# A two-branch attention kernel: a quarter of x loaded by a transposing DMA, and the first value projections moved behind the first scores

## The chip, the cores and the metric

The kernel runs on one core of a Trainium2 chip. The core has a matrix engine (TensorE, PE in the profile; its loads of stationary operands are listed apart as PEld), a vector engine (VectorE, DVE), an engine for activation functions (ScalarE, ACT), a general engine (GpSimd, POOL) and an engine that here only issues DMAs (SyncE, SP). Each engine works through its own list of instructions in order, and they wait for one another by semaphores. The metric is the device time of one execution in microseconds; smaller is better.

## What is computed

All of it takes one input `x` of 2048 rows and 512 columns in bf16. Branch A is full softmax attention with 32 heads of 16 columns. Branch B is attention over 8 earlier positions, 2 apart. A gate mixes both row by row.

```python
q, k, v = split(x @ wqkv)                      # 32 heads of 16 columns, A and B with weights of their own
a = softmax(q @ k.T * 16 ** -0.5) @ v @ wo     # branch A: 2048 keys for every query
b = softmax(q . k[pos - 2 * w] * 16 ** -0.5, w = 0..7) @ v[pos - 2 * w] @ wo   # branch B, masked where pos < 2 w
g = sigmoid((x * gate_w).sum(-1))
out = g * a + (1 - g) * b
```

Branch A's scores are 32 x 2048 x 2048 numbers, and each of them needs an exponential.

## The kernel before

**Units, periods and rings.** Scores are made transposed: a unit is one head, 128 keys and 512 queries, that is a tile of 128 x 512 in one PSUM bank. There are 32 heads x 16 key tiles x 4 query chunks = 2048 units. A period is four heads (a head group) and one query chunk, 64 units; there are 32 periods. TensorE writes three units into one ring buffer (`rA`) and two into the other (`rB`), in turns; ScalarE takes the exponential of a whole buffer in one instruction and writes bf16 (`pT`); TensorE multiplies these with the values (`vp_all`) into one accumulator bank (`acc`), which VectorE copies out (`accS`) when a period is over. An instruction of 128x1536 in the profile is an exponential of three units, one of 128x1024 of two.

**Three engines share the exponentials.** A unit can also go to VectorE, which makes the exponential in four passes over integer bits (`dve_unit`: `ta`, `ta`, `ta`, `pd`), or to GpSimd after a copy by VectorE (`pool_unit`: `psc`, `pd`). Such a unit sits in one of two banks called `w`, which the projections use as well.

**The order is made by a planner.** The class `Plan` (lines 52 to 292) is a list scheduler that runs while the program is built. Each job is a generator that asks for an engine, a priority and an assumed duration; the planner starts, at each step, the ready request that can start first, and so writes the order of every engine's list. The hardware then follows these lists and real semaphores. Two constants of it matter here. `limit` (line 185) says until when ScalarE has work, less `refill` (0.4 us); `fits` (line 218) lets a job of lower priority onto TensorE only if it ends within that limit, plus an allowance that grows with the job's waiting time by `RAMP` (0.006 us for each us after `CALM`). Where TensorE would sit idle, `idle_fill` (line 150) puts matmuls with zero weights (fillers: `acc<-ident,z`), which change no result.

**Loading x.** SP issues x in four chunks of 512 rows into `xr` (lines 398 to 407), the last chunk in two halves, with a piece of the query weights between; then the value weights `wv`, the rest of the key and query weights, and the weights of branch B. One piece of the key weights is issued by ScalarE. `x_half` (line 544) then turns half a chunk: eight TensorE transposes of 128 x 128 into a PSUM bank `s`, and one copy into `xT` by VectorE or ScalarE. The table `XDVE` (line 484) says which, and `XARR` (line 485) gives the planner assumed times of arrival. `xT` holds x with its 512 columns on the partitions and feeds every projection.

**The start.** With `xT` of a chunk, `k_job` (line 571) makes the keys of the first head group for that chunk (for the last chunk in two halves); VectorE takes the largest key magnitudes (`kmax_all`), ScalarE writes the keys (`kt_all`). When all five maxima are there, `sel_job` (line 618) makes `selk`, one more TensorE matmul subtracts a bound from the queries (in `q_job`, line 773), and VectorE writes the queries `qt`. Then the first ring can be written. The values of heads 0 to 7 are made by four value jobs (`v_job`, line 741), each of 16 matmuls and one VectorE cast, which `v_group` (line 1632) spawns. On line 1652 they are spawned with no event to wait for, at priority 3. All later value groups wait for the start of a period (`ev_start`).

Of the kernel before, what the change touches and what calls it, by code (L numbers as in the profile page):

```python
# [23 lines left out]
QW = 512  # L24
# [27 lines left out]
class Plan:  # L52
# [13 lines left out]
    held = {"job": 0}  # L66
    streamed = deque()
    cap_job = 2
    refill = 0.4
    patience = 6.0  # L70

    def resource(self, name, n):
# [106 lines left out]

    DEFER = 0.0  # L180
    coming = 0.0
    RAMP = 0.006
    CALM = 4.0

    def limit(self, st):
# [32 lines left out]
    def fits(self, x, st):  # L218
# [3 lines left out]
        give = self.EARLY if st < self.TEARLY else 0.0  # L222
        return st + x[4] - self.limit(st) <= max(give, self.RAMP * (st - x[7] - self.CALM))

# [71 lines left out]
def kernel(  # L296
# [12 lines left out]
    x2d = A_x.flatten_outer_dims()  # L309
    out2d = out.flatten_outer_dims()  # L310
    S, D = x2d.shape
    assert D == 512 and S == 2048
    NT = S // 128
    NC = S // QW
# [41 lines left out]
    SP = Chained(nc.sync, "sp")  # L356
# [16 lines left out]
    xT = const.tile([128, DC, S], BF16, name="xT")  # L373
# [24 lines left out]
    def load_x(t0, n):  # L398
        SP.dma_start(out=xr[t0 // 8][:, t0 // 4 % 2, t0 % 4:t0 % 4 + n],
                     in_=x2d[t0 * 128:(t0 + n) * 128, :].rearrange("(t p) n -> p t n", p=128))  # L400
# [2 lines left out]
    load_x(4, 4)  # L403
    SP.dma_start(out=wqr[:, :, 0:128], in_=a_w3[:, :, 0:128])
    load_x(8, 4)
    load_x(12, 2)
    load_x(14, 2)
    SP.dma_start(out=wv[:], in_=a_w3[:, :, 2 * D:3 * D])
    SP.dma_start(out=wkr[:, :, 128:D], in_=a_w3[:, :, D + 128:2 * D])
    SP.dma_start(out=wqr[:, :, 128:D], in_=a_w3[:, :, 128:D])  # L410
# [70 lines left out]
    THIN = 0.40  # L481
    KRP = 4
    QRP = 3
    XDVE = ((1, 0), (1, 0), (1, 1), (0, 1))
    XARR = ((5.8, 5.8), (7.2, 7.2), (9.3, 9.3), (9.9, 10.6))
    WARR = (4.8, 8.0)
    GP = 4.5
    BB = 3
# [24 lines left out]
    ev_x = [Event() for _ in range(NC)]  # L513
# [7 lines left out]
    ev_start = [Event() for _ in range(NP)]  # L521
# [16 lines left out]

    def x_job(sc):
        left = [2]  # L540
        for hf in range(2):
            yield ("spawn", x_half(sc, hf, left))

    def x_half(sc, hf, left):
        yield ("delay", XARR[sc][hf])
        w = Bank("s")

        def tr(s):
            P.thin = 0.16
            w.open(s, [128, DC, 256], BF16)  # L550
            for tt in range(2):
                for c in range(DC):
                    PE.transpose(out=w.t[:, c, tt * 128:(tt + 1) * 128],
                                 in_=xr[sc // 2][:, sc % 2, 2 * hf + tt, c * 128:(c + 1) * 128], identity=ident[:])
        yield ("pe", 0, 0.45, tr, "s")
        dst = xT[:, :, sc * QW + hf * 256:sc * QW + (hf + 1) * 256]
        if XDVE[sc][hf]:
            yield ("dve", 1, 0.70, lambda: V.tensor_copy(out=dst, in_=w.t[:]))
        else:
            yield ("act", 0, 1.02, lambda: A.copy(out=dst, in_=w.t[:]))  # L560
        yield w.close()
        left[0] -= 1
        if left[0] == 0:
            yield ("set", ev_x[sc])
# [176 lines left out]
    def v_job(h0, h1, tb, TB, rel, prio):  # L741
        n = (h1 - h0) * DH
        if rel is not None:
            yield ("wait", rel)
        for sc in range(tb * 128 // QW, -(-(tb + TB) * 128 // QW)):
            yield ("wait", ev_x[sc])
        w = Bank()

        def pe(t0, t1):
            def f(s=None):  # L750
                if t0 == 0:
                    w.open(s, [128, TB, n])
                for tt in range(t0, t1):
                    for c in range(DC):
                        mm(w.t[:, tt, :], xT[:, c, (tb + tt) * 128:(tb + tt + 1) * 128],
                           wv[:, c, h0 * DH:h1 * DH], c == 0, c == DC - 1)
                P.thin = (t1 - t0) * (one - 4 * n / 2400.0)
            return f
        step = TB if TB < 8 else TB // 2
        one = 4 * max(0.0555, n / 2400.0)  # L760
        for t0 in range(0, TB, step):
            yield ("pe", GO if t0 else prio, one * step + SW, pe(t0, t0 + step)) + (("w",) if t0 == 0 else ())
        yield ("dve", prio, VP, lambda: V.tensor_copy(out=vp_all[:, tb:tb + TB, h0:h1, 0:DH],
                                                      in_=w.t[:].rearrange("p t (h d) -> p t h d", d=DH)))
        yield w.close()
        for t in range(tb, tb + TB):
            for i in range(h0 // 4, h1 // 4):
                yield ("set", ev_v[(i, t)])
                v_left[0] -= 1
# [3 lines left out]
    def q_job(p, rel, prio):  # L773
        c_, i = periods[p]
        if rel is not None:
            yield ("wait", rel)
        yield ("wait", ev_x[c_])
        yield ("wait", ev_wq)
        if p > 0:
            yield ("wait", ev_sel[i])  # L780
        w = Bank()

        def pe(s):
            w.open(s, [128, QW])
            for c in range(DC):
                mm(w.t[:], wqp[:, c, i].rearrange("p j d -> p (j d)"), xT[:, c, c_ * QW:(c_ + 1) * QW],
                   c == 0, c == DC - 1)
        yield ("pe", prio, 4 * MM + SW, pe, "w")
        st = {}

        def absq():
            st["a"] = work.tile([128, QW], BF16, name="absq", tag="absq", bufs=1)
            hi = w.t[:].bitcast(I16).rearrange("p (n two) -> p n two", two=2)[:, :, 1]
            V.tensor_scalar(out=st["a"][:].bitcast(I16), in0=hi, scalar1=0x7FFF, scalar2=None, op0=ALU.bitwise_and)
        if p == 0:
            def absa():
                st["a"] = work.tile([128, QW], BF16, name="absq", tag="absq", bufs=1)
                A.activation(out=st["a"][:], in_=w.t[:], func=ACT.Abs)
            yield ("act", 0.2, 0.69, absa)
        else:  # L800
            yield ("dve", prio, VP, absq)
        yield ("wait", ev_sel[i])
        yield ("pe", GO, MM + SW, lambda: mm(w.t[:], selk_all[:, i, :], st["a"][:], False, True,
                                               skip_group_check=True))

        def evac():
            qt = work.tile([128, QW], BF16, name="qt", tag="qt", bufs=3)
            V.tensor_scalar(out=qt[:], in0=w.t[:], scalar1=QSC, scalar2=qbias[:, 0:1], op0=ALU.mult, op1=ALU.add)
            qt_tiles[p] = qt
        yield ("dve", prio, VP + 0.06, evac)  # L810
        yield w.close()
        yield ("set", ev_q[p])
# [819 lines left out]
    def v_group(h0, h1, rel, prio):  # L1632
        n = (h1 - h0) * DH
        TB = 512 // n
        for tb in range(0, NT, TB):
            P.spawn(v_job(h0, h1, tb, TB, rel, prio + 0.01 * tb))
# [5 lines left out]
    for sc in range(NC):  # L1642
        P.spawn(x_job(sc))
# [5 lines left out]
        P.spawn(k_job(0, NC - 1, None, 1.5, hf))  # L1649
    P.spawn(sel_job(0, 1.5))  # L1650
    P.spawn(q_job(0, None, 1.6))
    v_group(0, 8, None, 3)
    P.spawn(act_stream())
    P.spawn(g_job(GP))
    P.spawn(psc_job(ev_lent), 16.0)
# [79 lines left out]
```

## Time and profile before

Three timed runs took 845.38, 846.5 and 847.3 us, a median of 846.5 us. The profiled execution took 844.47 us, of which 842.7 us are the span of its instructions.

| engine | busy us | share of the span | instructions |
|---|---|---|---|
| PE | 743.3 | 88% | 5798 |
| DVE | 768.6 | 91% | 1333 |
| ACT | 825.7 | 98% | 750 |
| POOL | 731.0 | 87% | 740 |

The first exponential of a ring starts at 17.76 us. The loads of the first 21 us keep the 16 DMA engines busy; after that DMA is busy for a quarter of the time on average. TensorE's granted clock is at full speed in nearly all slices of the page. A busy TensorE is not one at its peak, since its matmuls overlap and since fillers count as busy.

### The profile page before, as it was taken

The numbers are of one execution on the slowest core, as the hardware profiler recorded it, in microseconds if no ns is written. First come the engines' busy times: TensorE is split into PE (matmuls) and PEld (weight loads), VectorE is DVE, ScalarE is ACT, GpSimd is POOL, SyncE is SP. The second block draws the span as 40 slices with busy tenths as digits, with TensorE's granted clock in tenths as the row PEclk, the third lists the DMA queues.
The fourth block names the chain that finished last, engine by engine and source line by source line (L and its number), as shares of the span: only waits on it lengthen the run. The fifth ranks groups of instructions, "written<-read, shape, count | busy, mean of one in ns | idle before, by whom it ended". The sixth has DMA issues, their size and how long they took to land.

```text
span 842.7 us, 15724 instructions
## 1 busy us (share of the span) xinstructions
PE 743.3 (88%) x5798; PEld 266.4 (32%) x5854; DVE 768.6 (91%) x1333; ACT 825.7 (98%) x750; POOL 731.0 (87%) x740
## 2 busy tenths in 40 slices
PE   9999998988898888888899898888898898888897
PEld 5423432333233323332333232332233332232222
DVE  5799999999999999999987999999999989998887
ACT  5999999999999999999999999999999999999996
POOL 2678679998999999999899999999989898978891
PEclk9999999999999999999999999999999999999999
DMA  9003240604243312230233240402212222110000
GB/s 296 7 14 107 89 132 22 208 22 109 92 135 123 98 53 64 75 110 10 70 89 94 64 142 21 131 14 73 84 33 82 69 87 77 26 57 14 8 1 26
DMA packets 72590, 63.85 MB, mean 76 GB/s; under 512 B 20528, under 2 KB 69168, under 8 KB 72512
## 3 DMA queue, kind: packets, MB, share of 16 engines
q1 hardware_dynamic: 71312, 62.57, 24.6%
q8 instruction: 46, 0.75, 0.4%
q10 hardware_dynamic: 1200, 0.26, 0.2%
q14 instruction: 32, 0.26, 0.1%
HBM read 46.14 MB, written 12.62 MB: 70 GB/s over the span
## 4 chain that ended last, share of the span: by engine, by line
ACT 73%; issue 20%; PE 7%; DVE 0%; POOL 0%; ACTq 0%; POOLq 0%
ACT pT L350 71%; PE acc L350 2%; PE ring L350 2%; PE w L350 2%; ACT lg L350 1%; PE s L350 1%; PE e L350 0%; DVE vp_all L350 0%; DVE qt L350 0%; ACT osc L350 0%; POOL ident masks.py:199 0%; ACT e L350 0%; POOL identf masks.py:197 0%; ACTq L350 0%; POOL ident masks.py:197 0%
## 5 line engine op out<-in xcount | busy, mean ns | idle before, releaser
L350 ACT ACTIVATE pT<-ring 128x1536 bf16<-128x1536 f32 x717 | 815.3, 1425 | 2.5 <-PE ring L350 1.8
L350 PE MATMUL ring<-qt,kt_all 32*128 32x512 bf16 x1857 | 286.9, 381 | 87.4 <-ACT pT L350 74.5
L350 DVE SCALAR_TENSOR_TENSOR ta<-ta,w 128x512 f32<-128x512 f32 x476 | 317.2, 681 | 6.1
L350 POOL TENSOR_TENSOR prod<-prod 128x512 f32<-128x512 f32 (+1 forms) x208 | 240.4, 1166 | 5.8
L350 PE MATMUL acc<-pT,vp_all 128*17 128x512 bf16 x1792 | 221.7, 384 | 2.7 <-DVE accS L350 2.4
L350 PEld LDWEIGHTS <-kt_all 32*128 32x128 bf16 x2113 | 114.2, 91 | 337.4 <-issue 325.3
L350 DVE TENSOR_SCALAR ta<-w 128x512 f32<-128x512 uint16 x238 | 162.6, 686 | 37.0 <-PE w L350 34.6
L350 PE MATMUL acc<-ident,z 128*17 128x512 bf16 (+5 forms) x741 | 185.5, 335 | 1.6 <-POOL ident masks.py:199 1.4
L350 DVE SCALAR_TENSOR_TENSOR pd<-ta,w 128x512 uint16<-128x512 f32 x238 | 160.5, 680 | 2.9
L350 POOL TENSOR_TENSOR prod<-ksh,qb 128x512 f32<-128x512 bf16 x128 | 144.8, 1156 | 8.7 <-DMA ksh<-kv_scr 6.4
L350 POOL TENSOR_TENSOR prod<-vsh,lg 128x512 f32<-128x512 bf16 x128 | 136.7, 1098 | 2.4
L350 PE MATMUL w<-qt,kt_all 32*128 32x512 bf16 x256 | 96.4, 383 | 0.1
L350 PE MATMUL acc<-pd,vp_all 128*17 128x512 bf16 x256 | 85.8, 382 | 0.0
L350 PEld LDWEIGHTS <-z 128*17 128x17 bf16 (+1 forms) x749 | 52.5, 91 | 67.8 <-issue 40.6
L350 PEld LDWEIGHTS <-vp_all 128*17 128x17 bf16 x2048 | 40.5, 87 | 93.4 <-issue 93.0
L350 POOL TENSOR_TENSOR psc<-psc 128x512 f32<-128x512 f32 x54 | 64.4, 1193 | 4.2
L350 PE MATMUL w<-bw,xT 128*128 128x512 bf16 x167 | 48.4, 382 | 1.4
L350 POOL TENSOR_SCALAR psc<-psc 128x512 f32<-128x512 uint16 (+1 forms) x36 | 22.2, 618 | 27.8 <-DVE psc L350 24.8
L350 PEld LDWEIGHTS <-xT 128*128 128x128 bf16 x448 | 31.3, 98 | 27.5 <-issue 14.0
L350 POOL TENSOR_TENSOR lg<-lg,mx 128x256 f32<-128x256 f32 x16 | 10.1, 629 | 22.3 <-DVE mx L350 22.3
L350 DVE COPY accS<-acc 128x512 f32<-128x512 f32 (+1 forms) x33 | 22.0, 668 | 1.5 <-PE acc L350 1.4
L350 DVE CAST kvs<-w 128x512 bf16<-128x512 f32 x32 | 21.8, 682 | 1.1 <-PE w L350 1.1
(108 smaller groups left out, 454.3 us busy)
## 6 DMA issues: line engine op xcount, KB each, us to landing
ksh<-kv_scr SPq DMA_DIRECT2D x16, 1024.0 KB
vsh<-kv_scr SPq DMA_DIRECT2D x16, 1024.0 KB
kv_scr<-kvs SPq DMA_DIRECT2D x16, 256.0 KB
kt_all<-k_scr SPq DMA_DIRECT2D x6, 512.0 KB
q_scr<-qpk SPq DMA_DIRECT2D x24, 128.0 KB
qt<-q_scr SPq DMA_DIRECT2D x24, 128.0 KB
out_dram<-osb SPq DMA_DIRECT2D x14, 128.0 KB
xr<-in_A_x_dram SPq DMA_DIRECT2D x3, 512.0 KB
```

Source lines behind the costliest of these rows:

```text
L350: return chain_on(self._key, f(*a, **k))
```

## The change

The last 512 rows of x are no longer loaded into `xr` and turned by TensorE. One transposing DMA, issued by SP in the place of the two half loads, writes them straight into `xT`; for that chunk the planner is told to assume an arrival at 12.6 us. The value jobs of heads 0 to 7 now wait for the event that marks the start of the first period, so they come behind the first scores in the planner's order. Two constants of the planner change: `refill` from 0.4 to 0.52 and `RAMP` from 0.006 to 0.01.

```diff
-    refill = 0.4
+    refill = 0.52
...
-    RAMP = 0.006
+    RAMP = 0.01
...
     load_x(8, 4)
-    load_x(12, 2)
-    load_x(14, 2)
+    SP.dma_start_transpose(out=xT[:, :, 3 * QW:S], in_=x2d[3 * QW:S, :])
     SP.dma_start(out=wv[:], in_=a_w3[:, :, 2 * D:3 * D])
...
-    XDVE = ((1, 0), (1, 0), (1, 1), (0, 1))
-    XARR = ((5.8, 5.8), (7.2, 7.2), (9.3, 9.3), (9.9, 10.6))
+    XDVE = ((1, 0), (1, 0), (1, 1))
+    XARR = ((5.8, 5.8), (7.2, 7.2), (9.3, 9.3), (12.6, 12.6))
...
     def x_job(sc):
         left = [2]
+        if sc == NC - 1:
+            yield ("delay", XARR[sc][0])
+            yield ("set", ev_x[sc])
+            return
         for hf in range(2):
...
-    v_group(0, 8, None, 3)
+    v_group(0, 8, ev_start[0], 3)
```

## The prediction

> **What bounds the kernel now.** I read the page first: busy shares, then the chain that ended last, then the costliest groups. (Columns of a group: its form and count | busy time, mean ns of one | idle before it.)
>
> ```profile
> PE 743.3 (88%) x5798; PEld 266.4 (32%) x5854; DVE 768.6 (91%) x1333; ACT 825.7 (98%) x750; POOL 731.0 (87%) x740
> ACT 73%; issue 20%; PE 7%; DVE 0%; POOL 0%; ACTq 0%; POOLq 0%
> L350 ACT ACTIVATE pT<-ring 128x1536 bf16<-128x1536 f32 x717 | 815.3, 1425 | 2.5 <-PE ring L350 1.8
> ```
>
> ScalarE is 98% busy, 815.3 of its 825.7 us with the 717 exponentials of the score ring, and these wait 2.5 us in all. So the span is three parts: the head up to the first exponential, the exponentials with their gaps, and the tail after the last. Three answers give the parts: ScalarE's timeline, and the exponentials' busy time in chosen stretches (columns: stretch, length, PE busy, ACT busy, clock, DMA share, GB/s).
>
> ```profile
> 17.76 17.32 ACT L350 ACTIVATE pT<-ring 128x1536 bf16<-128x1536 f32 x15 [1.79 <-PE ring L350]
> 836.75 0.37 ACT L350 COPY oT<-e 128x256 bf16<-128x256 bf16 x1 [2.59 <-PE e L350]
> 17.76:34.89 17.13, 3.94 (x35) 17.13 (x15) 1.00 0.23 74
> 747.82:834.16 86.34, 24.14 (x190) 86.13 (x77) 0.98 0.04 12
> ```
>
> Head 17.76 us; exponentials 17.76 to 834.16 = 816.40 us; tail 842.7 - 834.16 = 8.5 us. The pace comes from clean stretches: 38 exponentials (19 pairs of a three-unit and a two-unit one, a unit being 512 columns) between two small ACT operations at 167.24 and 210.11 take 42.87 us, 2.256 us a pair; 15 (8 long, 7 short) take 17.13 us, so a long one costs 17.13 - 7 x 2.256 = 1.34 us and a short one 0.915. The program before has 358 long and 359 short ones: 358 x 1.34 + 359 x 0.915 = 808.2 (a fit of 0.427 a unit plus 0.0615 an instruction gives 808.7). Sixteen `lg` exponentials at 0.31 between neighbours add 5.0, the gate's 0.1. Sum 813.8; the other 2.6 us are small gaps. The largest lies at the last change of accumulator: 76 exponentials from 747.82 should take 37 x 2.256 + 2 x 0.915 = 85.3 and take 86.3, and there TensorE's granted clock falls (clock third from the end):
>
> ```profile
> 811.00:814.00 3.00, 2.28 (x21) 0.65 (x19) 3.00 (x6) 3.00 (x4) 2.75 (x4) 0.84 0.00 0
> 814.00:817.00 3.00, 3.00 (x20) 1.15 (x21) 2.93 (x7) 2.79 (x3) 2.75 (x4) 0.59 0.00 0
> ```
>
> The head's own chain is in TensorE's and VectorE's timelines (start, length, operation, count).
>
> ```profile
> 9.94 2.13 PE L350 MATMUL s<-ident,xr 128*128 128x128 bf16 x32
> 11.90 2.76 PE L350 MATMUL s<-xT,wkp 128*128 128x512 bf16 x16
> 14.81 1.07 PE L350 MATMUL w<-wv,xT 128*128 128x128 bf16 x16
> 17.32 0.39 PE L350 MATMUL ring<-qt,kt_all 32*128 32x512 bf16 x3
> 13.83 1.35 DVE L350 TENSOR_REDUCE kmax_all<-s 128x1 f32<-128x512 f32 x3 [0.17 <-PE s L350]
> 15.41 0.25 DVE L350 TENSOR_SCALAR selk_all<-selq,kmax 128x128 bf16<-128x128 bf16 x1
> 15.91 0.69 DVE L350 CAST vp_all<-w 128x512 bf16<-128x512 f32 x1 [0.25 <-PE w L350]
> 16.52 0.74 DVE L350 TENSOR_SCALAR qt<-w,qbias 128x512 bf16<-128x512 f32 x1
> ```
>
> Transposes of x, keys, maxima, `selk`, then a value group on TensorE and its cast on VectorE ahead of `qt`, then the first ring, whose exponential starts 0.44 later.
>
> **What the skill says.** No x load is transposed by DMA before, but outputs are. The Trainium skill, Advanced Engine Details and Errata, section X-Bar Transpose (TRN2): such DMAs are as fast as regular ones, 350 to 400 GB/s; its page DMA: Bandwidth & Descriptors, section Latency and other measured facts, gives 261 GB/s where the middle dimension isn't contiguous. The trace is lower. A transpose of 128 KB alone on the queues (40 slices of 0.2 us from 128.0):
>
> ```profile
> 128.22 1.20 SPq L350 DMA_TRANSPOSE oT<-otok  x1
> GB/s 0 0 0 0 0 0 0 164 220 210 62 0 0 0 0 0 0 0 0 0 0 0 0 0 0 0 0 0 0 0 0 0 0 0 0 0 0 0 0 0
> ```
>
> It holds SP for 1.20 us, moves nothing for those, then 210 to 220 GB/s. I use 220. That source lies in SBUF, the new one in HBM; 150 and 261 are my bounds. For the clock, the skill's TensorE: Matmul & The Clock Gate (What's actually happening) says that an idle window of about 3.4 us throttles TensorE; the trace agrees so far that the clock fell just where TensorE was 2.28 of 3 us busy.
>
> **Part 1: the transposing load.** It removes two loads, 16 TensorE transposes, one xT copy on ScalarE and one on VectorE. The 32 transposes of 9.94 to 11.90 become 16, so TensorE is 1.0 us ahead. Then I walk on by durations of the rows. Keys of chunk 1: 10.95 to 11.8. Keys of chunk 2 wait for both copies of that chunk, both on VectorE, which in the trace end at 11.9: 12.0 to 12.9. Keys of chunk 3, in two halves of 0.45 (16 matmuls took 2.76, so four 256-wide ones half of 0.87): 12.9 to 13.8, if the transposed data is there. The last maximum ends 0.5 to 0.6 later as before (14.66 to 15.18), at 14.4; `selk` 0.48 after that, as before, at 14.9 against 15.66. Gain so far 0.8.
>
> Is the data there at 12.9? DMA rates in 1 us slices of the first 40 us:
>
> ```profile
> GB/s 0 25 104 325 349 315 91 295 385 361 347 349 327 333 376 400 387 399 368 350 346 99 10 0 0 16 0 0 0 0 0 0 0 0 0 0 0 16 0 0
> ```
>
> To 9.0 us they sum to 1889 KB. Ahead of the transpose stand 131 + 524 + 524 + 131 + 524 = 1834 KB and some 50 KB of instructions, so its turn comes at 9.0; being issued from about 2.9, its 1.2 us of preparation, even four times that (4.8), lie beside those transfers. 524 KB at 220 GB/s are 2.4 us: 11.4. From the last byte to TensorE's first use was 0.5 (second load: 1182 KB at 6.7, use at 7.23) to 1.2 us (first: 4.6, use at 5.80); 0.9 gives 12.3, no wait. At 261 it is 11.9; at 150, 13.4 and 0.5 lost. Queued behind it on SP are `wv`, the other weights and the `zpad` row: `wv` started at 5.54; if SP is held until 10, its 524 KB end by 12.5 at the 340 GB/s of the trace, and it is needed at 16.5. The rest is used tens of microseconds later. Queue delays cost nothing.
>
> **Part 2: values after the first scores.** In the changed program's order the first value group stands behind the first ring. It frees `selk`'s matmul from the group that ended at 15.88, and `qt` from a cast until 16.6. So `selk`'s matmul is at 14.9 to 15.4, `qt` 15.4 to 16.15, ring 16.2, first exponential 16.65: 1.1 before 17.76 in all. Ring, group of 1.0, ring is the pattern that stood at 17.32 to 19.03 and left no gap in 17.13 us; one more such slot is hidden behind the exponentials.
>
> **Part 3: the two planner constants.** `refill` and `RAMP` change no operation's length, but with the new head they reorder every engine's list. Counted there: 359 long and 359 short exponentials, 1795 units against 1792; VectorE has 236 units against 238, GpSimd 17 against 18. That puts 0.427 + 0.915 = 1.34 us onto ScalarE, the bound; VectorE's and GpSimd's relief lies beside it. TensorE has 26 more fillers, put where the plan has it idle: cost nothing. Gaps: 2.6 now. I can bound them only: 0 below (nothing waits), 4.6 above (two more dips like that at 811, of 1.0 each). At the last change of accumulator the new order has ten ring matmuls and five 512-wide fillers where it had six and two, which keeps TensorE busier; I take that dip as mostly gone: 1.9, so -0.7. Tail: behind the last exponential stand 7 matmuls into `acc` for 4, one more wave of 0.21, and two fewer `bwo` ones at the very end: +0.15 (bounds -0.3 and +0.5).
>
> **Sum.** -1.1 + 1.34 - 0.7 + 0.15 = -0.3: span 842.4. The profiled execution took 844.47 device us for its 842.7; the timed ones 845.38 to 847.3, median 846.5, so 3.8 over the span: 846.2.
>
> **Rivals.**
> Faster: the gaps nearly vanish, because the larger `refill` holds back TensorE jobs that end close to the moment ScalarE runs dry. For it: the 26 extra fillers show a slacker TensorE plan. Against: most pieces already run at the floor (67 exponentials from 49.03 in 75.42 us, 33 x 2.256 + 0.915 = 75.36). With 0.6 left: -1.1 + 1.34 - 2.0 + 0.15 = -1.6, and up to 0.4 more if `qt` is sooner: 844.7. The floor with no gap is 16.65 + 808.7 + 1.34 + 5.1 + 8.65 = 840.4, or 844.2.
> Slower: the transpose from HBM lands late. Keys of chunk 3 stand in TensorE's list with everything after them, so each microsecond past 12.9 goes straight to the first exponential. From 14.9 on (105 GB/s) the kernel is over 0.2% slower; at 15.4, which is 16 blocks issued one after another at 0.3 us each only from 9.0 on with 1.6 to the use, it is -0.3 + 2.5 = +2.2: 848.7. For it: nothing here shows an HBM source, and SP is held 1.2 us for a quarter of the bytes. Against: the preparation can lie under the earlier loads.
> Also slower: two more clock dips than now, -1.1 + 1.34 + 2.0 + 0.15 = +2.4: 848.9. That the change does nothing is excluded: 16 transposes are gone and the ring stands first.
>
> **Chances.** Measurement tells this kernel from no change at about 0.2%, 1.7 us. Forecast (within): 0.42. Faster: 0.32. Slower: 0.26, of which late transpose 0.16 and dips 0.10. The forecast's own range is 844.8 to 847.7. The range for 8 in 10 takes in the faster case with 0.4 for scatter, and the slower ones at their named size: 843.8 to 848.9.
>
> **What would show it.** First exponential at 16.65 (right), or above 17.76 with TensorE waiting for the DMA of xT before the chunk 3 keys (wrong). 718 exponentials, sum of their busy time up by 1.3. From the first to the last exponential 817.1 (816.4 + 1.34 - 0.7). No dip of the clock near the end. Wrong if dips appear at other changes of accumulator, or if the sum of gaps leaves 0.6 to 3.5.

## The result, and the profile after

The changed kernel takes 849.57 us (849.07 to 849.78, four runs) against 846.5: a ratio of 1.0036, 95% interval 1.0019 to 1.0054. It is slower, and outside the predicted range of 843.8 to 848.9. The profiled execution spans 848.0 us against 842.7; in the runs of this study the device time is 1.73 to 2.06 us above the span, 1.78 in those four.

First the page of the changed kernel: busy shares, the chain that ended last, and the group of the exponentials (busy time, mean ns | idle before it).

```profile
PE 751.2 (89%) x5813; PEld 267.4 (32%) x5864; DVE 762.1 (90%) x1323; ACT 826.6 (97%) x750; POOL 725.3 (86%) x734
...
ACT 66%; issue 20%; PE 10%; DVE 4%; POOL 0%; ACTq 0%; POOLq 0%
...
L350 ACT ACTIVATE pT<-ring 128x1536 bf16<-128x1536 f32 x718 | 817.2, 1408 | 5.2 <-PE acc L350 2.4
```

There are 718 exponentials, as forecast. They wait 5.2 us where they waited 2.5, the largest part (2.4) for TensorE's `acc`; TensorE's share of the chain rose from 7 to 10%. ScalarE's timeline gives the bounds of the three parts, and one window its busy time in the middle part (columns: stretch, length, PE, PEld, DVE, ACT, POOL busy, clock, DMA share, GB/s).

```profile
17.88 19.53 ACT L350 ACTIVATE pT<-ring 128x1536 bf16<-128x1536 f32 x17 [1.43 <-PE ring L350]
...
818.81 20.45 ACT L350 ACTIVATE pT<-ring 128x1536 bf16<-128x1536 f32 x18 [1.28 <-PE acc L350]
```

```profile
17.88:839.26 821.38, 730.42 (x5683) 257.75 (x5731) 749.59 (x1284) 817.61 (x735) 719.52 (x720) 1.00 0.24 72
```

Head 17.88 (before 17.76), middle 839.26 - 17.88 = 821.38 (816.40), tail 8.74 (8.54). The 5.3 us are in the middle. By the prediction's own measure the work of these exponentials is 813.8 + 1.34 = 815.1, which leaves 6.2 us of gaps against 2.6. (That measure is an estimate, good to about 0.5 us: the prediction's two sums for the exponentials before are 808.2 and 808.7, and its fit as printed gives 809.3. The difference between two kernels hardly depends on it.) ScalarE idles 821.38 - 817.61 = 3.77 us of the middle, against 0.76 before; the rest of the gaps, 2.4 and 1.8 us, is time in which ScalarE is busy, at a pace a little below that of the clean stretch.

The head did shorten, but it started later. TensorE's timeline from the start (start, length, operation, count), of the changed kernel:

```profile
1.44 5.82 PE L350 MATMUL acc<-ident,z 128*32 128x512 bf16 x17 [1.44 <-POOL ident masks.py:199]
7.20 1.07 PE L350 MATMUL s<-ident,xr 128*128 128x128 bf16 x16
...
12.15 2.99 PE L350 MATMUL s<-xT,wkp 128*128 128x512 bf16 x16
...
17.44 0.39 PE L350 MATMUL ring<-qt,kt_all 32*128 32x512 bf16 x3
17.76 1.07 PE L350 MATMUL w<-wv,xT 128*128 128x128 bf16 x16
```

and the same first lines of the kernel before:

```profile
1.44 4.43 PE L350 MATMUL acc<-ident,z 128*32 128x512 bf16 x17 [1.44 <-POOL ident masks.py:199]
5.80 1.07 PE L350 MATMUL s<-ident,xr 128*128 128x128 bf16 x16
```

The 17 fillers ahead of the first transposes took 5.82 us in one execution and 4.43 in the other. A filler of 512 columns took 0.63 us at first and 0.38 later, and the change, TensorE's full clock, came at about 7.0 us here and 4.0 there (the trace's first record of full clock stands at 6.93 and 4.10; ahead of it the clock column reads 1.00 without a record). A second profile of the changed kernel has them done sooner, first transposes at 6.16, first exponential at 16.84. From first transposes to first exponential it is 10.68 us in both, 11.96 and 11.71 in two profiles of before: 1.0 to 1.3 shorter. The keys at 12.15 wait for no DMA. The load can be told apart in the trace by its packets, 2048 of 256 bytes that the kernel before doesn't have: they move from 8.3 to 11.25 us, and the prediction had 9.0 to 11.4. This is SP's queue:

```profile
3.29 6.47 SPq L350 DMA_TRANSPOSE xT<-in_A_x_dram  x1
9.81 0.58 SPq L350 DMA_DIRECT2D wv<-in_A_wqkv_dram  x1
```

Where ScalarE idles in the middle (the bracket is the idle time and its releaser; `818.81` above is the last of them):

```profile
59.16 8.23 ACT L350 ACTIVATE pT<-ring 128x1536 bf16<-128x1536 f32 x7 [0.34 <-PE ring L350]
67.57 7.01 ACT L350 ACTIVATE pT<-ring 128x1024 bf16<-128x1024 f32 x6 [0.18 <-PE ring L350]
75.28 14.58 ACT L350 ACTIVATE pT<-ring 128x1024 bf16<-128x1024 f32 x13 [0.70 <-PE acc L350]
90.39 15.12 ACT L350 ACTIVATE pT<-ring 128x1536 bf16<-128x1536 f32 x13 [0.53 <-PE w L350]
105.73 27.23 ACT L350 ACTIVATE pT<-ring 128x1024 bf16<-128x1024 f32 x24 [0.22 <-PE w L350]
153.76 22.71 ACT L350 ACTIVATE pT<-ring 128x1024 bf16<-128x1024 f32 x20 [0.17 <-PE acc L350]
...
489.00 28.14 ACT L350 ACTIVATE pT<-ring 128x1024 bf16<-128x1024 f32 x25 [0.23 <-PE acc L350]
```

These eight make 3.65 of the 3.77 us. The second profile has all eight at the same distance from its first exponential, and equal within 0.01 us, so they belong to the instruction lists, not to chance. The kernel before has one, 0.32 us, 31 us after its first exponential.

### The profile page after: what moved, and what is told of

Its sections match the earlier page's. It is cut to its first block, busy times and chain, and to the rows that moved or that the text cites. A ratio compares the mean times of both kernels' runs of the same rounds, so it can differ in the third digit from the quotient of the medians.

```text
span 848.0 us, 15723 instructions
## 1 busy us (share of the span) xinstructions
PE 751.2 (89%) x5813; PEld 267.4 (32%) x5864; DVE 762.1 (90%) x1323; ACT 826.6 (97%) x750; POOL 725.3 (86%) x734
## 4 chain that ended last, share of the span: by engine, by line
ACT 66%; issue 20%; PE 10%; DVE 4%; POOL 0%; ACTq 0%; POOLq 0%
ACT pT L350 65%; PE w L350 4%; PE acc L350 3%; PE ring L350 3%; DVE ta L350 2%; ACT lg L350 1%; PE s L350 1%; DVE pd L350 1%; PE e L350 0%; DVE psc L350 0%; DVE xT L350 0%; DVE d L350 0%; DVE kt_all L350 0%; DVE osb L350 0%; DVE omg L350 0%
## 5 line engine op out<-in xcount | busy, mean ns | idle before, releaser
L350 PE MATMUL acc<-ident,z 128*17 128x512 bf16 (+3 forms) x770 | 193.6, 338 | 1.4 <-POOL ident masks.py:199 1.4
L350 PE MATMUL acc<-pd,vp_all 128*17 128x512 bf16 x253 | 82.0, 380 | 0.0
L350 POOL TENSOR_TENSOR psc<-psc 128x512 f32<-128x512 f32 x51 | 60.8, 1193 | 3.9
```

What stands on the lines that cost most here:

```text
L350: return chain_on(self._key, f(*a, **k))
```

## The experiments

Each was compared with the kernel before, in four groups of runs. "Clock" is TensorE's mean granted clock; below, a run "at full clock" is one of at least 0.998. It has to be told apart because two thirds of the runs of before, 24 of 35 in the first group, lie below 0.998 and take 846.8 us, while the other 11 take 845.25 (medians; in the other groups before takes 845.16, 844.92 and 845.26 at full clock, so that 0.3 us between groups mean nothing). All ten timed runs of the changed kernel are at full clock.

| kernel | time us | ratio (95%) | at full clock us (runs) |
|---|---|---|---|
| before, run again | 845.72 | 0.9989 (0.9982, 0.9997) | 844.9 (8) |
| load alone | 845.60 | 0.9993 (0.9980, 1.0005) | 843.9 (4) |
| value wait alone | 850.14 | 1.0044 (1.0029, 1.0059) | 848.8 (1) |
| load and value wait, old constants | 847.84 | 1.0019 (1.0012, 1.0026) | 847.75 (16) |
| the same and RAMP | 847.94 | 1.0018 (1.0010, 1.0026) | 847.9 (15) |
| the same and refill | 848.58 | 1.0024 (1.0017, 1.0031) | 848.6 (13) |
| load and constants, no value wait | 846.78 | 1.0018 (1.0009, 1.0028) | 846.4 (11) |
| the change, again | 849.45 | 1.0034 (1.0021, 1.0047) | 849.45 (6) |
| the change with refill 0.51 | 849.12 | 1.0042 (1.0026, 1.0058) | 848.75 (4) |
| two exchanges in TensorE's list | 849.64 | 1.0038 (1.0023, 1.0053) | 849.6 (5) |
| a wider exchange | 850.10 | 1.0041 (1.0026, 1.0055) | 850.1 (6) |
| load, ten fillers at the start | 844.95 | 0.9974 (0.9964, 0.9984) | 844.0 (4) |
| before, ten fillers at the start | 845.86 | 1.0002 (0.9989, 1.0015) | 844.3 (5) |
| load, ten fillers, values moved by hand | 846.85 | 1.0005 (0.9995, 1.0015) | 845.1 (7) |

And the parts read from each profile: head from the first transposes of x to the first exponential, the middle, its exponentials, the gaps over their work (813.8 for before's 717; 815.1 for 718; 815.6 where a 512-column one makes 719; 816.1 with refill 0.51, where a two-unit one does), ScalarE's idle time in it, and the tail.

| kernel | head | middle | exps | gaps | idle | tail | clock |
|---|---|---|---|---|---|---|---|
| before | 11.96 | 816.40 | 717 | 2.6 | 0.76 | 8.5 | 0.998 |
| before, again | 11.71 | 815.88 | 717 | 2.1 | 0.55 | 8.5 | 1.000 |
| load alone | 11.04 | 818.52 | 717 | 4.7 | 2.66 | 8.5 | 0.994 |
| value wait alone | 11.35 | 822.16 | 719 | 6.5 | 3.89 | 9.0 | 0.992 |
| load and value wait | 10.68 | 819.25 | 719 | 3.6 | 1.33 | 9.0 | 1.000 |
| and RAMP | 10.69 | 819.82 | 719 | 4.2 | 1.79 | 8.9 | 1.000 |
| and refill | 10.84 | 820.21 | 719 | 4.6 | 2.27 | 8.9 | 0.999 |
| load and constants | 11.04 | 818.51 | 719 | 2.9 | 1.13 | 8.6 | 1.000 |
| the change | 10.68 | 821.38 | 718 | 6.2 | 3.77 | 8.7 | 0.999 |
| refill 0.51 | 10.68 | 820.72 | 719 | 4.7 | 2.38 | 9.0 | 0.999 |

### Each part alone

The load alone: the edits of the load, `XDVE`, `XARR` and `x_job`, in the kernel before. Its list differs from before only ahead of the first ring.

> Part 1 of the change alone: the transposing load, the value jobs and both planner constants as before. Its lists differ from those before only ahead of the first ring (16 TensorE transposes and two copies fewer), 717 exponentials as before. Theory A (the planner's new lists cost the time, the load is good): 0.8 to 1.2 us faster than before, the stretch from the first to the last exponential 816 to 817 us. Theory B (the load costs the time, because it holds SP for 6.5 us and leaves holes in the DMA traffic): no gain or slower, the first exponential at 17.9 or later even where TensorE's clock is up early. Theory C (the two profiles differ by when TensorE's clock came up, 4.0 us before and 7.0 after): the first exponential moves by up to 1.4 us from run to run of one kernel, at the same lists.

The value wait alone, in the kernel before:

```diff
-    v_group(0, 8, None, 3)
+    v_group(0, 8, ev_start[0], 3)
```

> Part 2 alone: the value jobs wait for the first period, x is loaded as before, constants as before. The planner writes other lists: 718 exponentials (1795 units), VectorE 235 and GpSimd 17. Theory A: head 0.4 us sooner, 1.3 us more exponential work, and gaps of 2 to 5 us between exponentials: 1 to 4 us slower than before. Theory B: about +0.9 (the 1.3 less 0.4), no more gaps than before.

The changed kernel with the old constants:

```diff
-    refill = 0.52
+    refill = 0.4
-    RAMP = 0.01
+    RAMP = 0.006
```

> Parts 1 and 2 without part 3: the changed kernel with refill 0.4 and RAMP 0.006. Its lists are those of the kernel with part 2 alone but for the head. Theory A: 0.8 to 1.2 us faster than the kernel with part 2 alone, and against the whole change it tells what the constants cost: if they are the cause, 2 us or more faster than the whole change; if the value wait alone throws the lists about, the same as the whole change. Theory B: as slow as the whole change, since the load is in it.

The changed kernel again, unchanged:

> The whole change once more. Theory A: about 3 us slower than before, first to last exponential again 821 us, whatever the head does. Theory C: its first exponential can come at 16.5 to 17.9, depending on when TensorE's clock comes up.

The load did what it was meant to: head 11.04, and at full clock 843.9 us (four runs) against 845.25, 1.35 less; over all runs the gain is within the noise. Of the 2.66 us of idle time in its profile, 2.0 lie where the clock falls. In windows around them (columns as above, clock third from the end) the load alone has

```profile
638.00:641.00 3.00, 2.92 (x16) 0.89 (x16) 1.52 (x5) 2.34 (x3) 2.92 (x3) 0.56 0.22 46
764.00:767.00 3.00, 3.00 (x17) 0.96 (x14) 2.16 (x5) 2.56 (x3) 2.92 (x4) 0.50 0.03 5
767.00:770.00 3.00, 3.00 (x16) 0.51 (x14) 2.38 (x6) 2.07 (x3) 2.40 (x2) 0.50 0.01 3
```

and before, run again, with the same list there:

```profile
638.00:641.00 3.00, 2.86 (x22) 0.98 (x20) 2.51 (x7) 3.00 (x4) 2.84 (x3) 1.00 0.06 12
764.00:767.00 3.00, 2.65 (x25) 1.07 (x20) 2.93 (x6) 3.00 (x4) 2.92 (x4) 1.00 0.01 3
767.00:770.00 3.00, 2.41 (x20) 0.70 (x20) 1.66 (x5) 3.00 (x4) 2.35 (x2) 1.00 0.00 0
```

So the middle of a run at 0.994 may not be set against one at 1.0: that would charge the load with 2.6 us, while its runs at full clock show none. The value wait is the dear part. Added to the load it takes another 0.36 us off the head and puts 3.4 us onto the middle against before run again (819.25 against 815.88): 1.83 of exponential work, because one more long exponential (1.34) and one of 512 columns (0.49 by the prediction's fit) come to ScalarE, and 1.5 of gaps. The tail is 0.5 longer. The value wait alone shows the same list in a run at 0.992: head 11.35, and a middle that the clock has stretched to 822.16. By these profiles it costs 3.5 us in all, by the times at full clock 3.9 (847.75 against 843.9).

### The two constants

Only `refill`, then only `RAMP`, as in the changed kernel, the other one old:

> The changed kernel with RAMP back at 0.006; load, value wait and refill 0.52 stay. Lists: 718 exponentials, 754 fillers, VectorE 235. If refill alone makes the gaps between exponentials (the plan believes TensorE jobs are harmless that are not), first to last exponential is 821 us or more, as with the whole change, against 819.25 with both old constants. If any new list brings gaps of its own by chance, it lies anywhere from 817 to 823 us, at places other than 75, 90 and 818 us.

> The changed kernel with refill back at 0.4; load, value wait and RAMP 0.01 stay. Lists: 718 exponentials, 734 fillers. If RAMP is the cause (it lets TensorE jobs that have waited run past the point where ScalarE runs dry), gaps as with the whole change and 821 us from the first to the last exponential; if refill is, about 819. By chance of the list: anywhere from 817 to 823.

Each on its own costs something, 0.96 and 0.57 us of the middle; by time it is 0.85 and 0.15 at full clock, so `RAMP` alone is hardly told from nothing. Neither reached the 821 us that was set as the sign of a sole cause. `refill` brings, in the place of one of 0.68, the six idle spells of 59 to 154 us, all of them and at the same places; a spell like that of 489 comes with `RAMP`. The largest, 1.28 us at 818.81, is in neither: among these lists it needs both. So the two are no sum of single prices. The constants without the value wait (its line back to `None`) and the changed kernel with `refill` 0.51:

> The changed kernel with its first value group planned as before, ahead of the first scores: the load and the two constants, without the value wait. Its list has 718 exponentials (+1.34 us, as the changed kernel). Theory A (the constants as such reorder TensorE's work so that it comes late for the ring): head about 11.04 us from the first transposes as with the load alone, and from the first to the last exponential at least 820.4, as 819.3 + 1.1 or more; time 848.5 or above. Theory B (each setting gives its own list, good or bad, and only the pairing with the value wait is a bad one): the middle can be anything, 816.5 to 822; a middle below 818.5 and a time below 847 speak for it.

> The changed kernel with refill 0.51 for 0.52: the same parts, another list (719 exponentials, 1797 units against 1795, so 0.9 to 1.8 us more of them). Theory A (refill above 0.5 in general costs gaps): middle 822 to 823.5, as 821.4 with the longer exponentials, gaps about 6. Theory B (what the constant does is a matter of each single list): gaps that differ by 1 us or more from 6.2, either way, and at other places than 57.98 to 152.6 and 818.8.

Without the value wait the same constants leave gaps of 2.9 and three small spells of idle time in the whole middle:

```profile
48.80 75.64 ACT L350 ACTIVATE pT<-ring 128x1024 bf16<-128x1024 f32 x67 [0.32 <-PE acc L350]
...
306.49 27.23 ACT L350 ACTIVATE pT<-ring 128x1024 bf16<-128x1024 f32 x24 [0.32 <-PE acc L350]
486.68 10.06 ACT L350 ACTIVATE pT<-ring 128x1024 bf16<-128x1024 f32 x9 [0.33 <-PE acc L350]
```

Their cost there is the exponential work, +1.83, and 0.8 of gaps. The middle, 818.51, is on the edge that was set for theory B, and the time below its 847: it speaks for B more than for A. With 0.51 the middle, 820.72, is below what A had set. The six early spells stay as they are, within 0.01 us, which B had not expected, while those of 489.00 and 818.81 are gone: B holds for the late part of the list only. A step of 0.01 in a constant moved 1.3 us of idle time and one exponential; at full clock the time fell by 0.7 us only, since the exponentials' work grew by 0.9.

### Is it the order, or TensorE's time?

At 88.92 the changed kernel has a projection of 1.04 us just ahead of a ring, and ScalarE then idles 0.53 until 90.39. That looked like a wrong order. Two kernels put it to the test, with every other instruction of TensorE where it was and the lists of the other engines unchanged.

```diff
+            def go():
                 for c in range(DC):
                     mm(w.t[:], wqr[:, c, 128 * (b + 1):128 * (b + 2)], ...)
+            (put_off if b == 0 and c_ == 0 else now)(go, True)
...
                         qk_mm(ring[:, s_, :], p_, t, j)
+                while late:
+                    late.pop(0)()
```

> The changed kernel with two pairs of neighbours exchanged in TensorE's list by hand, and every other instruction where it was: the third wkr projection (at 73.09 in the changed kernel's profile) and the first wqr projection (at 88.92) each go behind the ring that they stand ahead of. Theory A (the planner put a projection of 1.0 us ahead of a ring that ScalarE needed at once; the order is the cause): the idle 0.53 us at 90.39 is gone, as that exponential waits for nothing but its ring. The idle 0.70 at 75.28 may stay, because the trace names the accumulation at 74.58 as its releaser, and that still stands behind the projection. Middle 820.2 to 820.9 for 821.4. Theory B (TensorE is short of time there, whatever the order): the idle time comes back within the next few exponentials and the middle stays at 821.2 to 821.5.

> As the version before, but the wkr projection goes behind the accumulation that follows the ring too (four matmuls), just ahead of the next ring. Theory A: both the 0.70 and the 0.53 us are gone, middle 820.0 to 820.3, time 1.1 to 1.3 us below the changed kernel, 848.3. Theory B: idle time reappears behind them and the middle stays above 821.

Theory A fell. TensorE with the exchange at that place,

```profile
88.51 0.39 PE L350 MATMUL ring<-qt,kt_all 32*128 32x512 bf16 x3
88.83 1.04 PE L350 MATMUL w<-xT,wqr 128*128 128x512 bf16 x4
89.80 0.39 PE L350 MATMUL w<-qt,kt_all 32*128 32x512 bf16 x1
90.12 0.60 PE L350 MATMUL acc<-pT,vp_all 128*17 128x512 bf16 x5
90.65 0.39 PE L350 MATMUL ring<-qt,kt_all 32*128 32x512 bf16 x2
```

and ScalarE:

```profile
74.79 15.93 ACT L350 ACTIVATE pT<-ring 128x1024 bf16<-128x1024 f32 x14 [0.92 <-PE acc L350]
91.14 1.02 ACT L350 ACTIVATE pT<-ring 128x1024 bf16<-128x1024 f32 x1 [0.42 <-PE ring L350]
92.44 12.86 ACT L350 ACTIVATE pT<-ring 128x1536 bf16<-128x1536 f32 x11 [0.28 <-PE ring L350]
```

The ring is served early, and the next two are late: 0.42 and 0.28 for 0.53, and 0.92 for 0.70. The middle is 821.84, and 822.13 with the wider exchange (0.28 and 0.49 in place of the 0.70), against 821.38; that is above the bounds of B too. At these places a projection that is moved only moves the wait. What else stands there is seen in TensorE's groups from 38 to 76 us after the first exponential (busy us, mean ns | idle before), of before run again:

```profile
L350 PE MATMUL ring<-qt,kt_all 32*128 32x512 bf16 x88 | 13.5, 382 | 2.1 <-ACT pT L350 1.9
...
L350 PE MATMUL w<-bw,xT 128*128 128x512 bf16 x12 | 3.1, 382 | 0.0
L350 PE MATMUL acc<-ident,z 128*17 128x512 bf16 x8 | 3.1, 384 | 0.0
L350 PE MATMUL w<-wv,xT 128*128 128x128 bf16 x32 | 2.1, 220 | 0.0
L350 PE MATMUL w<-xT,wqr 128*128 128x512 bf16 x8 | 2.1, 382 | 0.0
L350 PE MATMUL w<-xT,wkr 128*128 128x512 bf16 x8 | 2.1, 380 | 0.1
L350 PE MATMUL w<-xT,wqp 128*128 128x512 bf16 x8 | 2.0, 377 | 0.2 <-DVE psc L350 0.2
```

and of the changed kernel:

```profile
L350 PE MATMUL ring<-qt,kt_all 32*128 32x512 bf16 x82 | 12.8, 382 | 1.5 <-ACT pT L350 1.3
...
L350 PE MATMUL w<-xT,wkr 128*128 128x512 bf16 x15 | 4.1, 380 | 0.3 <-DVE psc L350 0.2
L350 PE MATMUL acc<-ident,z 128*17 128x512 bf16 x11 | 4.1, 385 | 0.0
...
L350 PE MATMUL w<-bw,xT 128*128 128x512 bf16 x8 | 2.1, 382 | 0.0
L350 PE MATMUL w<-xT,wkp 128*128 128x512 bf16 x7 | 2.0, 380 | 0.2 <-DVE pd L350 0.2
L350 PE MATMUL w<-xT,wqp 128*128 128x512 bf16 x7 | 2.0, 378 | 0.3
...
L350 PE MATMUL w<-wv,xT 128*128 128x128 bf16 x16 | 1.1, 220 | 0.0
...
L350 PE MATMUL w<-xT,wqr 128*128 128x512 bf16 x3 | 1.0, 383 | 0.1
```

Projections of keys and queries take 9.1 us for 6.2 (nine groups of four matmuls for six; a trace lacks some matmul records, so 32 are listed), values and `bw` 3.2 for 5.2: 0.9 us more work that is not scores, and about 6 ring matmuls fewer in the same 38 us. TensorE's wait for ScalarE ahead of a ring falls from 1.9 to 1.3 us. ScalarE's idle time in the stretch is 1.8 us (0.34, 0.18, 0.70, 0.53), twice the extra work. Two things speak against a plain lack of TensorE's time. Fillers of all sizes take 7.2 us there for 5.9, so the list has room. And the kernel with the old constants has nearly as many projections (8.8 us) and a smaller wait for ScalarE, 1.0, but less idle time, 1.1 us, 0.68 of it in one spell that ends at 64.12. So the extra projections arrive with the value wait, and how much idle time they cost depends on where `refill` puts them.

The trace of the changed kernel says where: in seven of the eight spells a projection or a value group of 1.0 us stands between the ring that ScalarE waits for and the one ahead of it. In three of them it starts late itself, as VectorE has not yet cleared the `w` bank that it needs, by 0.17, 0.23 and 0.36 us (ahead of the spells that end at 59.16, 75.28 and 105.73):

```profile
73.09 1.02 PE L350 MATMUL w<-xT,wkr 128*128 128x512 bf16 x4 [0.23 <-DVE psc L350]
```

Whether the late banks or the bunched projections are the cause was not tested, nor why the planner draws just these jobs together.

### A shorter start, and the value group by hand

Ten fillers for seventeen ahead of the first transposes, added to the load alone, and to the kernel before:

```diff
-            for a in range(0, n, QW):
+            for a in range(0, n if P.now > 7.0 else min(n, 6 * QW), QW):
```

> The transposing load alone (values and constants as before), with 10 instead of 17 fillers ahead of the first transposes of x; every other instruction of the three engines' lists the same. Theory C (the head waits for fillers that run at the slow clock): the first transposes start at 5.8 us in each run instead of 5.8 to 7.2, the first exponential at 16.9 instead of 17.7, and the kernel is 0.3 to 1.0 us faster than the one with the load alone (845.6). Rival: the clock comes up later with fewer fillers, and transposes at the slow clock give the gain back: no difference.

> The kernel before with ten fillers at the start for seventeen and nothing else. Theory A (fillers that run at the low clock until about 7 us hold back the first transposes of x): first transposes at 5.3 to 5.8 in every run, and the time 0.3 to 1.2 us below before, 845.4 to 846.2. Theory B (what made the short start faster was only together with the transposing load): time within 0.3 us of before. If TensorE's full clock comes later with fewer fillers, the head is longer instead and the time up to 1 us above before.

First transposes came at 5.23 and 5.49, but ran at the low clock or waited for the next chunk of x. Load and short start together are the best kernel measured, 844.95 us, ratio 0.9974. The interval is clear of 1, but so is that of before against itself in the same group, 0.9989; against those runs (845.72) the lead is 0.8 us. How much of that the short start gives is not settled: at full clock it is level with the load alone (844.0 and 843.9, four runs each), and on the kernel before it makes no difference (1.0002).

Last, the value wait without the planner: the first value group and its cast go behind the first ring by hand, every later list unchanged. And the kernel before, run again as a yardstick.

> The transposing load and ten fillers at the start for seventeen, as in the version run before, and the first value group with its cast put behind the first ring by hand, the rest of every engine's list left as it was. Theory A (the value wait is worth 0.36 to 0.6 us of the head, and its cost came from the new list alone): first exponential 0.3 to 0.6 earlier against the first transposes than without it, 717 exponentials, no new gap, middle 816 to 817 where the clock does not dip, time 844.5. Theory B (the cast, now behind qt on VectorE and the group behind the ring, is missed by the first accumulations or holds the second ring): a gap of 0.3 us or more within the first five exponentials, time 845 or above.

> The kernel before once more. Theory C: its head is 11.96 us from the first transposes of x to the first exponential as in the first profile, but the first transposes start anywhere from 5.8 to 7.2 us; first to last exponential 815.4 us plus about 1.0 for each dip of TensorE's clock near the end of the run.

The yardstick reads 0.9989: comparisons are good to about 0.1%. By hand the value group cost more than it saved (845.1 at full clock, against 844.0 without it). TensorE's timeline after the first ring,

```profile
16.92 1.07 PE L350 MATMUL w<-wv,xT 128*128 128x128 bf16 x16
18.77 1.05 PE L350 MATMUL w<-wv,xT 128*128 128x128 bf16 x16 [0.78 <-DVE vp_all L350]
19.76 0.39 PE L350 MATMUL ring<-qt,kt_all 32*128 32x512 bf16 x2
```

and ScalarE's:

```profile
17.04 1.45 ACT L350 ACTIVATE pT<-ring 128x1536 bf16<-128x1536 f32 x1 [1.67 <-PE ring L350]
20.19 16.00 ACT L350 ACTIVATE pT<-ring 128x1024 bf16<-128x1024 f32 x14 [1.70 <-PE ring L350]
```

The slot behind the first ring already held a value group. Two stand there now, the second waits for the first one's cast, and ScalarE idles 1.70 us. To delay one group without this gap, every later one has to move a slot back; that is what the planner's new list does, and its gaps come further on.

## Why the prediction was wrong

- **Head, -1.1: right.** Measured from the first transposes it is 1.3 or 1.0, by the profile of before (11.96 or 11.71 to 10.68): the load 0.9 or 0.7, the value wait 0.36. That the profile of after shows its first exponential at 17.88, not 16.65, is the late clock of that execution (first transposes 1.4 us later); the second profile has 16.84. I had taken one execution's start as fixed, and it was the earliest of thirteen profiles with 17 fillers.
- **Late transposing load: right that it doesn't matter.** Its bytes landed at 11.25 for 11.4. (Of the 1.2 us from last byte to first use that the prediction read for the first load, a part was fillers: with ten of them, the first transposes came at 5.23 instead of 5.80.) SP was held 6.47 us, more than the longest preparation considered (4.8), but only until 9.76, where the prediction had 10; `wv` was issued at 9.81, TensorE waits for no DMA.
- **Exponential work, +1.34: right**, 718 of them.
- **Tail, +0.15: right**, 8.54 to 8.74.
- **Gaps, 2.6 to 1.9: this step failed.** They are 6.2 in both profiles of the change, beyond the bound of 4.6 and the 3.5 above which the prediction called itself wrong. The missing 4.3 us are the whole error of the middle (821.38 against 817.1). I had bounded the gaps by dips of the clock, since those were what before showed, and had read 26 more fillers as slack. In the new list the gaps have nothing to do with the clock, which is full from 6.93 us until after the last exponential. All eight spells that make up 3.65 of the 3.77 us of idle time end with TensorE's instructions: TensorE comes late for ScalarE. That the gaps come with the new list, from the value wait and more so with the constants, is shown by the runs. That an exchange of neighbours cures none of it is shown for two of the eight. Why TensorE is late at these places, bunched projections or `w` banks that VectorE clears late, stays open.
- **"That dip as mostly gone": wrong with its sign.** At the last change of accumulator the clock did stay up, as it also did with the old list in before run again; but the largest idle spell, 1.28, ends at 818.81 there. The profile names the `acc` matmuls as its releaser, behind the doubled rings; the five fillers, 1.24 us from 818.57 on, stand behind them. Whether the doubled rings or the accumulations are to blame was not taken apart.
- **3.8 from span to time: mis-sized by 2.0.** Device time is 1.78 over the span. The other 2.0 set the timed runs of before apart from the profiled one: 0.8 even at full clock (845.25 against 844.47), where the early start of the profiled one may have its part, and 1.25 more from there to the median, in runs at a lower clock. The changed kernel shows no such runs among its ten. The span was missed by 5.6 us, 1.2 of it the late start, 4.3 the middle, 0.1 the tail; the 2.0 hid so much of it that the time was missed by 3.4 only. It also is why the change costs 3 us in the comparison, and 4.2 where both are at full clock (849.45 against 845.25).

By parts at full clock, added in this order: load -1.35, value wait +3.9, constants +1.7, in sum +4.2. In the other order the constants cost 2.5 (846.4 against 843.9) and the value wait 3.05, so the parts have no price of their own. None of the rivals had this mechanism; the slower ones came near the time (848.7 and 848.9) by causes that did not occur.

## What to carry to other kernels

When the engine that sets the pace is 98% busy and another stands at 88%, work that is moved out of an idle head is not free: it can push other work to moments at which the second engine has no slack, even if the stretch around them has some, and at two such places an exchange of neighbours only moved the wait. If a planner writes the order, treat every edit that reaches it as a new order: look, stretch by stretch, at what the new list puts between the jobs that feed the bounding engine, before pricing its gaps from the old profile. And take the start of a profile, and the step from span to time, from more than one execution.

## What the runs showed of the hardware

- A transposing load of 512 KB from HBM held SP's queue for 6.47 us (6.43 in the load alone); a transposing DMA of 128 KB out of SBUF held it 1.20. The Trainium skill, Advanced Engine Details and Errata, section X-Bar Transpose (TRN2), puts such DMAs level with regular ones at 350 to 400 GB/s. In both profiles of the change the load's own packets take 2.8 to 3.0 us from first to last, a mean of 177 to 188 GB/s; from 10 to 11 us, with nothing else on the queues, they move at 290.
- TensorE's full clock began between 4.1 and 7.2 us after the start from one execution to the next, with the same 17 fillers ahead, and moved the first transposes from 5.80 to 7.35 us over thirteen profiles.
- The same list at the same place ran at a clock of 1.00 in one execution and 0.50 in another (764 to 767 us). The Trainium skill, TensorE: Matmul & The Clock Gate, section What's actually happening, ties the fall to an idle window of about 3.4 us; no such window is seen here: before run again, TensorE was busy 2.65 and 2.41 of 3 us there and kept its clock. At the place of the fall that the prediction took for agreement (811 to 814 us) before run again was busy 2.28 of 3 us too, at a clock of 1.00.
- Six of the profiles have twelve such dips ahead of their last exponential. Each lasts 3.41 us or twice that, and begins a whole multiple of 3.413 us after the clock first rose in its execution (in the load alone at 5.79 us; the first dip begins at 637.25, 185 times 3.413 later). In the 3.41 us just before a dip TensorE was busy for 0.66 to 0.72 of the time; other such stretches, as light, were followed by none. Whether a list dips may thus depend on how its light stretches fall on that grid; no run here tests it.
